# Loads 3 to 4 items ahead, shared score buffers and identity products at the start of an attention and mixture kernel

## The chip, the cores and the metric

One core of one Trainium2 chip. The metric is the device time of one execution in microseconds (us), the median of three runs. Smaller is better.

## The reference

Three layers run one after the other, in float32:

1. Attention for 4 batches of 8 heads, 576 tokens, 64 values for each head. The score of query i and key j is q.k/8 plus a bias, the negative of the decay accumulated from j to i: `bias = -(cum[i] - cum[j])` with `cum = cumsum(max(s, 0))`, capped at 0. Keys after the query are masked, then softmax and the product with v.
2. A gated layer on the 2304 tokens of width 512: `h = (x @ w1) * (x @ w2) @ w3`, then `h @ w_out`, with 1024 inner columns.
3. A soft mixture of 8 experts with 4 slots each: logits against `phi`, a softmax over tokens that forms the slots, a two-layer expert for each slot, a softmax over slots that spreads the results back over the tokens.

## The kernel before

The attention is cut into 32 "items". Items 0 to 7 are the 8 heads of the first batch with query tiles 0 to 2 (64, 128 and 128 queries), items 8 to 15 the same heads with tiles 3 and 4, and items 16 to 31 one head each of the other batches with all five tiles.

The way of an item n: `att_fetch` (line 267) loads q and k, already transposed, into a tile "raw" of two buffers (`NRW`), by the DMAs of lines 278, 279 or 281. `att_prep` (line 284) loads the values v of a pair of heads (line 291, tag "v", two buffers) when the head's number is odd, and four rows that carry the decay into partitions 64 to 67 of the same tile, so that one product yields score and bias. Items 0 and 1 (`NDIR`) get these rows from SBUF (line 300), later ones from a DRAM copy (line 302) that `decay_store` (line 164) has written. Items 0 to 15 (`NF32`) multiply the raw tile in float32; items from 16 on split it into two parts first, in tiles "qa" and "qb" of two buffers each, the same size as "raw". `att_scores` (line 318) makes the product of a query tile (line 334) in a PSUM tile of tag "sg" (four buffers), lets VectorE add the mask and take the row minimum of the scaled negative (line 337) and ScalarE take the exponential (line 342) into the score tile "sc" (three buffers, 1600 columns; tile i begins at column 64 i i, so that tiles 0 to 2 end at column 576). `att_norm` divides by the row sum (VectorE lines 351 and 352, GpSimd line 355). `att_transpose` turns the result on TensorE (lines 370 and 384) and ScalarE copies it out (lines 372 and 386). `att_pv` multiplies a pair of heads with v (through the helper at line 110), and the result is split into two parts of x (lines 419 and 420).

`glu_half` (line 426) multiplies x with w1 and w2 of one block of inner columns (products "gl", line 432). These weights arrive as 64-bit floats, "words": `fetch_words` (line 175, DMA at line 178, three buffers) loads 512 columns, `convert` turns them into 32-bit ones on ScalarE (line 186) and VectorE (lines 189, 190 and 193; another form uses 197, 198 and 201), and `load_words` splits them (ScalarE line 217, GpSimd line 218).

The order: `att_steps` (line 631) lists, for each step n, the scores of item n, the norm and transposes of n-1, the output product of the pair before when n is even, `att_prep` of n+1 and `att_fetch` of n+2. `weave` mixes these lists with the conversion steps and the gated layer's. The sync engine (SP), which issues nearly all loads, works strictly in this program order: a load that waits for its buffer holds back all that follows it. The other engines' instructions are put in order beforehand by a planner, and each engine then runs its own list in that order. Ahead of the steps, the loads of items 0 and 1 and of the first words, the decay rows, `att_prep(0)`, one more word load and the decay store are issued.

Of the kernel before, what the change touches and what calls it, by code (L numbers as in the profile page):

```python
# [10 lines left out]
F32 = mybir.dt.float32  # L11
# [10 lines left out]
P = 128  # L22
B, H, S, D = 4, 8, 576, 64
# [24 lines left out]
def attn_glu_softmoe_kernel(  # L48
# [14 lines left out]
    nc = tc.nc  # L63
# [16 lines left out]
    def psum(tag, name):  # L80
        return ps.tile([P, 512], F32, tag=tag, name=name, bufs=PB[tag])
# [37 lines left out]
    ident = cp.tile([P, P], F32, name="ident")  # L119
# [144 lines left out]
    hd = {}  # L264
    ITEMS = [(h, t) for t in ((0, 1, 2), (3, 4)) for h in range(H)] + [(h, (0, 1, 2, 3, 4)) for h in range(H, NH)]

    def att_fetch(n, ap):
        h, tiles = ITEMS[n]
        if h % 2 == 0:
            b, c = divmod(h // 2, H // 2)  # L270
            for blk, (_, nt, own) in enumerate(BLK):
                if own[0] in tiles:
                    x_t[b, blk, c] = xpl.tile([P, 2, nt], F32R, tag=f"x{blk}", name=f"x_{b}_{blk}_{c}", bufs=NX)
        q0, q1 = QT[tiles[0]][0], sum(QT[tiles[-1]])
        raw = ap.tile([P, 2, S], F32, tag="raw", name=f"raw_{n}", bufs=NRW)
        m = 64 if n < NF32 else P
        if q0:
            nc.sync.dma_start(raw[:m, 0, q0:q1], qk[h, 0, :m, q0:q1])
            nc.sync.dma_start(raw[:m, 1, :q1], qk[h, 1, :m, :q1])
        else:  # L280
            nc.sync.dma_start(raw[:m, :, :q1], qk[h, :, :m, :q1].rearrange("n p t -> p n t"))
        hd[n] = dict(raw=raw, q0=q0, q1=q1)

    def att_prep(n, ap):
        h, tiles = ITEMS[n]
        t = hd[n]
        raw, q0, q1 = t["raw"], t["q0"], t["q1"]
        if h % 2:
            vt = ap.tile([P, 9, 2, D], F32, tag="v", name=f"v_{n}", bufs=VB)
            nv = 2 * tiles[-1] + 1  # L290
            nc.sync.dma_start(vt[:, :nv], v[h // 2, :, :nv])
            t["v"] = hd[n - 1]["v"] = vt
        if n < NF32:
            rows = raw
        else:
            rows = ap.tile([P, 2, S], F32R, tag="qb", name=f"qb_{n}", bufs=QAB)
            qa = ap.tile([P, 2, S], F32R, tag="qa", name=f"qa_{n}", bufs=QAB)
        if n < NDIR:
            for a in range(2):
                nc.sync.dma_start(rows[64 + 2 * a : 66 + 2 * a, :, :q1].bitcast(F32), dec[a][h : h + 1, :, :, :q1])  # L300
        else:
            nc.sync.dma_start(rows[64:68, :, :q1].bitcast(F32), rows_d[h].rearrange("a b n t -> (a b) n t")[:, :, :q1])
        if n < NF32:
            t["mul"] = [rows[:68]]
            return
        rq, rk, qb = raw[:, 0], raw[:, 1], rows
        nc.vector.tensor_copy(qa[:, 0, q0:q1], rq[:, q0:q1])  # L307
        nc.scalar.dma_start(qb[0:64, 0, q0:q1].bitcast(F32), qa[0:64, 0, q0:q1].bitcast(F32))
        nc.vector.tensor_copy(qa[:, 1, :q1], rk[:, :q1])
        nc.gpsimd.tensor_tensor(  # L310
            out=qb[0:64, 1, :q1], in0=rk[0:64, :q1], in1=qa[0:64, 1, :q1].bitcast(F32), op=ALU.subtract
        )
        nc.gpsimd.tensor_tensor(  # L313
            out=qa[64:, 0, q0:q1], in0=rq[64:, q0:q1], in1=qa[64:, 0, q0:q1].bitcast(F32), op=ALU.subtract
        )
        t["mul"] = [qa, qb[:68]]

    def att_scores(n, i, ap):
        t, tiles = hd[n], ITEMS[n][1]
        if i == tiles[0]:  # L320
            t["nmax"] = sm.tile([P, 6], F32, tag="nmax", name=f"nmax_{n}")
            t["rsum"] = rsum_t[n % 3]
            t["sc"] = ap.tile([P, 1600], F32, tag="sc", name=f"sc_{n}", bufs=SCB)
        nmax, rsum, mul = t["nmax"], t["rsum"], t["mul"]
        q0, r = QT[i]
        W = q0 + r

        r = P
        sc = t["sc"][:, 64 * i * i : 64 * i * i + W]
        cuts = [(0, W)] if W <= 512 else [(0, W // 2), (W // 2, W)]  # L330
        for m, (a, z) in enumerate(cuts):
            pp = psum("sg", f"sc_ps_{n}_{i}_{m}")
            for x in mul:
                nc.tensor.matmul(pp[:r, : z - a], x[:, 0, q0 : q0 + r], x[:, 1, a:z], start=x is mul[0], stop=x is mul[-1])  # L334
            m0 = S - P if i == 0 else S - W + a
            last = m == len(cuts) - 1
            nc.vector.tensor_tensor_reduce(  # L337
                out=sc[:r, a:z], in0=pp[:r, : z - a], in1=hd["mask"][:r, m0 : m0 + z - a], scale=-0.125,
                scalar=3.0e38 if m == 0 else nmax[:r, 5:6], op0=ALU.add, op1=ALU.min,
                accum_out=nmax[:r, i : i + 1] if last else nmax[:r, 5:6],  # L340
            )
# [289 lines left out]
    def att_steps(ap):  # L631

        groups = [[] for _ in range(B + 1)]
        N = len(ITEMS)
        for n in range(N + 1):
            tiles = ITEMS[n][1] if n < N else ()
            old = [i for i in ITEMS[n - 1][1] if i] if 0 < n <= N else []
            sc = [(0.2 + 0.3 * i, lambda i=i, n=n: att_scores(n, i, ap)) for i in tiles]
            tr = [(0.2 + 0.3 * i, lambda i=i, n=n: att_transpose(n - 1, i, ap)) for i in old]
            norm = [(0, lambda n=n: att_norm(n - 1))] if 0 < n <= N else []  # L640
            prep = [(0, lambda n=n: att_prep(n + 1, ap))] if n + 1 < N else []
            if n + 2 < N:
                prep += [(0, lambda n=n: att_fetch(n + 2, ap))]
            blks = [k for k in range(2) if BLK[k][2][0] in ITEMS[n - 1][1]]
            pv = [(1.4, lambda n=n, k=k: att_pv(n - 2, k)) for k in blks] if n > 0 and n % 2 == 0 else []
            groups[min(B, max(0, (n - 1) // H))] += [
                *sc[:1], *norm, *sc[1:2], *prep, *sc[2:3], *tr[:1], *sc[3:4], *tr[1:2], *sc[4:], *tr[2:], *pv
            ]
        return groups
# [78 lines left out]
    with tc.tile_pool(name="att", bufs=1) as ap:  # L728
# [49 lines left out]
        prep = [(1, lambda k=k: load(k)) for k in range(2 * N0 + 2)]  # L778
# [323 lines left out]
```

## Time and profile before

| | |
|---|---|
| time, median of 3 runs | 574.28 us (573.58 to 574.37) |
| span of the profiled execution | 569.3 us |
| time outside the span, by the median | 5.0 us |
| TensorE (PE) busy | 519.9 us, 91% |
| VectorE (DVE) busy | 316.7 us, 56% |
| ScalarE (ACT) busy | 311.6 us, 55% |
| GpSimd (POOL) busy | 194.7 us, 34% |
| DMA | 118.04 MB, mean 207 GB/s |

The profile is one execution; its span runs from the first to the last instruction. The profile records no other time for that execution, so the 5.0 us are the difference to the median of the runs. Busy time counts instructions on each engine; PE's weight loads run beside its products. A busy share over the whole span mixes stages with different limits, so the rows further below are taken by stretch.

### The profile page before, as it was taken

The page shows a single profiled execution, that of the slowest core. Times are in us where ns is not written, and L with a number is a line of the kernel's source. Part 1 is how long each engine was busy: PE and PEld are TensorE (multiplying, and loading weights), DVE is VectorE, ACT ScalarE, POOL GpSimd, SP SyncE. Part 2 cuts the span into 40 slices and gives each one's busy share as a digit, 9 for nine tenths or more (in the row PEclk, how much of TensorE's full clock was granted, in tenths as well). Part 3 has the DMA queues.
Part 4 walks back from the last instruction along what each step waited for, and adds up shares of the span by engine and source line. Part 5 has one row for each costly group of instructions (what it writes and reads, how often), then busy time and mean ns, then how long its engine had stood idle before and what let it go on. Part 6 is the DMA issues. An engine that isn't in the chain of part 4 may idle for free.

```text
span 569.3 us, 11835 instructions
## 1 busy us (share of the span) xinstructions
PE 519.9 (91%) x4288; PEld 434.2 (76%) x4288; DVE 316.7 (56%) x966; ACT 311.6 (55%) x845; POOL 194.7 (34%) x247
## 2 busy tenths in 40 slices
PE   1886999788899999999899999999999999999993
PEld 1664788666788897989899879898888999853452
DVE  6558676769987376656565757456640311243333
ACT  4577667666876665845576667456833321321222
POOL 5447531526678456252255444333210000000000
PEclk9998999979999999999999999999999999999997
DMA  6557557657763353536556554465351996689976
GB/s 197 188 164 229 183 180 252 238 170 237 224 218 116 119 165 108 169 95 205 176 155 189 170 185 139 156 200 163 123 212 48 368 411 233 238 295 423 421 296 235
DMA packets 38810, 118.04 MB, mean 207 GB/s; under 512 B 4224, under 2 KB 10560, under 8 KB 35296
## 3 DMA queue, kind: packets, MB, share of 16 engines
q1 hardware_dynamic: 36832, 113.74, 57.9%
q10 hardware_dynamic: 1920, 3.54, 2.5%
q8 instruction: 34, 0.56, 0.4%
q14 instruction: 24, 0.20, 0.1%
HBM read 102.11 MB, written 11.60 MB: 200 GB/s over the span
## 4 chain that ended last, share of the span: by engine, by line
PE 38%; DMA 5%; DVE 4%; ACT 2%; issue 1%; POOL 0%; SPq 0%; DVEq 0%; POOLq 0%; ACTq 0%
PE gl L432 17%; DMA raw_w<-in_w 4%; PE x_ps L110 3%; PE o_ps L1003 3%; PE h_ps L965 3%; PE gn_ps L602 2%; PE sc_ps L334 2%; PE pt_ps L370 2%; PE z_ps L110 1%; DVE w_w L198 1%; PE ptd_ps L384 1%; PE y_ps L889 1%; PE lg L110 1%; DVE sc L337 1%; DVE w_w L201 1%
## 5 line engine op out<-in xcount | busy, mean ns | idle before, releaser
L432 PE MATMUL gl<-x,w12t 128*128 128x320 f32 (+1 forms) x1536 | 241.0, 307 | 4.2 <-DVE nmax L337 2.4
L432 PEld LDWEIGHTS gl<-x,w12t 128*128 128x128 f32 x1536 | 215.4, 194 | 12.8 <-DVE nmax L337 4.3
L342 ACT ACTIVATE sc<-sc,nmax 128x64 f32<-128x64 f32 (+4 forms) x160 | 89.8, 563 | 40.4 <-DVE nmax L337 38.7
L355 POOL TENSOR_SCALAR sc<-sc,rinv 128x64 f32<-128x64 f32 (+4 forms) x160 | 91.0, 585 | 56.7 <-DVE rinv L352 45.8
L313 POOL TENSOR_TENSOR qa<-raw,qa 64x576 fp32r<-64x576 f32 x24 | 36.9, 1536 | 145.5 <-DVE qa L307 134.0
L337 DVE CUSTOM_DVE_ANT_0 sc<-sc_ps,mask 128x64 f32<-128x64 f32 (+4 forms) x160 | 65.3, 424 | 35.6 <-PE sc_ps L334 32.8
L372 ACT COPY pt<-pt_ps 128x128 f32<-128x128 f32 (+3 forms) x128 | 52.4, 422 | 27.8 <-PE pt_ps L370 18.1
L370 PE MATMUL pt_ps<-ident,sc 128*128 128x128 f32 x320 | 56.6, 288 | 5.4 <-POOL sc L355 4.3
L370 PEld LDWEIGHTS pt_ps<-ident,sc 128*128 128x128 f32 x320 | 39.5, 146 | 16.7 <-POOL sc L355 7.7
L334 PE MATMUL sc_ps<-qa 128*128 128x64 f32 (+1 forms) x144 | 46.2, 334 | 5.3 <-DVE nmax L337 2.3
L334 PE MATMUL sc_ps<-raw 68*128 68x288 f32 (+4 forms) x96 | 33.8, 495 | 17.8 <-DMA raw<-rows 13.3
L438 ACT COPY a<-gl 128x256 f32<-128x256 f32 (+1 forms) x64 | 25.4, 397 | 38.4 <-PE gl L432 34.8
L110 PE MATMUL x_ps<-pt,v 128*64 128x256 f32 (+1 forms) x384 | 45.8, 352 | 0.0
L334 PE MATMUL sc_ps<-qb 68*128 68x64 f32 (+1 forms) x144 | 43.7, 307 | 0.7 <-issue 0.7
L310 POOL TENSOR_TENSOR qb<-raw,qa 64x576 fp32r<-64x576 f32 x24 | 38.0, 1582 | 2.2 <-issue 0.5
L974 POOL MEMSET ht<- 128x1024 f32 x2 | 1.9, 954 | 107.3 <-DVE ew L878 98.4
L334 PEld LDWEIGHTS sc_ps<-raw 68*128 68x128 f32 x96 | 19.5, 241 | 23.4 <-issue 12.4
L110 PEld LDWEIGHTS x_ps<-pt,v 128*64 128x64 f32 x384 | 31.1, 139 | 6.9 <-issue 0.9
L186 ACT ACTIVATE w_w<-raw_w 128x512 f32<-128x512 f32 x32 | 21.6, 674 | 23.5 <-DMA raw_w<-in_w 22.4
L420 DVE TENSOR_TENSOR x<-x_ps,x 128x320 fp32r<-128x320 f32 (+1 forms) x32 | 14.0, 453 | 36.5 <-ACT x L419 36.5
L334 PEld LDWEIGHTS sc_ps<-qa 128*128 128x128 f32 x144 | 27.5, 191 | 8.7 <-DVE nmax L337 4.1
L605 ACT COPY gn<-gn_ps 128x512 f32<-128x512 f32 x40 | 22.7, 582 | 15.2 <-PE gn_ps L602 14.8
(180 smaller groups left out, 786.5 us busy)
## 6 DMA issues: line engine op xcount, KB each, us to landing
ew<-in_ew SPq DMA_DIRECT2D x27, 1024.0 KB
raw_w<-in_w SPq DMA_DIRECT2D x32, 512.0 KB
raw<-in_qk SPq DMA_DIRECT2D x24, 576.0 KB
v<-in_v SPq DMA_DIRECT2D x16, 576.0 KB
raw_w3t<-in_w3t SPq DMA_DIRECT2D x16, 512.0 KB
raw_wot<-in_wot SPq DMA_DIRECT2D x8, 512.0 KB
raw_wo<-in_wo SPq DMA_DIRECT2D x8, 512.0 KB
w_d<-w_w SPq DMA_DIRECT2D x8, 512.0 KB
```

The source lines that it names most:

```text
L110: mm = nc.tensor.matmul(out_, lhs, rhs, start=start, stop=stop)
L310: nc.gpsimd.tensor_tensor(out=qb[0:64, 1, :q1], in0=rk[0:64, :q1], in1=qa[0:64, 1, :q1].bitcast(F32), op=ALU.subtract)
L313: nc.gpsimd.tensor_tensor(out=qa[64:, 0, q0:q1], in0=rq[64:, q0:q1], in1=qa[64:, 0, q0:q1].bitcast(F32), op=ALU.subtract)
L334: nc.tensor.matmul(pp[:r, : z - a], x[:, 0, q0 : q0 + r], x[:, 1, a:z], start=x is mul[0], stop=x is mul[-1])
L337: nc.vector.tensor_tensor_reduce(out=sc[:r, a:z], in0=pp[:r, : z - a], in1=hd["mask"][:r, m0 : m0 + z - a], scale=-0.125, scalar=3.0e38 if ...
L342: nc.scalar.activation(out=sc[:r, :W], in_=sc[:r, :W], func=AF.Exp, bias=nmax[:r, i : i + 1], scale=-1.0, accum_out=rsum[:r, i, 0:1],)
L355: nc.gpsimd.tensor_scalar(out=sc, in0=sc, scalar1=rinv[:, i : i + 1], scalar2=1.0, op0=ALU.mult, op1=ALU.mult)
L370: nc.tensor.transpose(tp[:, j * P : (j + 1) * P], sc[:, j * P : (j + 1) * P], ident)
L372: t["turned", i] = nc.scalar.copy(out=pt[:, p0 : p0 + step * (i - 1) + 1 : step], in_=tp[:, : i * P].rearrange("p (j q) -> p j q", q=P))
L432: nc.tensor.matmul(acc[:, :nt], w12_t[fc][:, wi, n, kc], x_t[b, blk, kc][:, xi], start=k == 0, stop=k == 3 * KC - 1)
L438: nc.scalar.copy(out=a_sb[:, :nt], in_=acc[:, :nt])
L605: st["turned", blk, k, h] = nc.scalar.copy(out=gn[:r, 4 * h : 4 * h + 4].rearrange("p c f -> p (c f)"), in_=tp[:r])
```

## The change

Items below 16 keep their raw tile in one of six buffers: those of "raw", "qa" and "qb" in turn. From the start, decay rows are loaded for items 0 to 2 and q and k for items 0 to 3 before the first step; step n then loads the rows of item n+3 and q and k of item n+4 (`FAR` = 3). From item 16 on the old distances hold. The load of the values becomes a function of its own and keeps its place. Among the first eight items, an even and an odd one share a score buffer, the odd one from column 800 on. Ahead of the scores of the first query tile of items 0 to 7, 20 and then 3 each products of the identity with itself are written into the first 128 columns of the PSUM tile that the scores then overwrite.

```
--- before.py
+++ after.py
@@ -83,7 +83,7 @@
 
     NW, NRAW, NG4, NX, NE_ = 8, 3, 4, 6, 11
     NRW, SCB, PTB, QAB, VB = 2, 3, 2, 2, 2
-    NF32, NDIR, ND = 16, 2, 1
+    NF32, NDIR, ND, FAR = 16, 2, 1, 3
 
     A1, CA, CB1, CB, GB1, GB, GC = 0.6, 8, 16, 26, 8, 16, 24
 
@@ -98,6 +98,8 @@
     ]
 
     GROUP = 1000
+
+    IDLE = (20, 3, 3, 3, 3, 3, 3, 3)
 
     CH, OT = ((3, 3, 1, 2), (1, 2, 3, 3)), "wwwweeee"
 
@@ -272,7 +274,8 @@
                 if own[0] in tiles:
                     x_t[b, blk, c] = xpl.tile([P, 2, nt], F32R, tag=f"x{blk}", name=f"x_{b}_{blk}_{c}", bufs=NX)
         q0, q1 = QT[tiles[0]][0], sum(QT[tiles[-1]])
-        raw = ap.tile([P, 2, S], F32, tag="raw", name=f"raw_{n}", bufs=NRW)
+        tag = ("raw", "qa", "qb")[n % 3] if n < NF32 else "raw"
+        raw = ap.tile([P, 2, S], F32, tag=tag, name=f"raw_{n}", bufs=NRW)
         m = 64 if n < NF32 else P
         if q0:
             nc.sync.dma_start(raw[:m, 0, q0:q1], qk[h, 0, :m, q0:q1])
@@ -281,15 +284,18 @@
             nc.sync.dma_start(raw[:m, :, :q1], qk[h, :, :m, :q1].rearrange("n p t -> p n t"))
         hd[n] = dict(raw=raw, q0=q0, q1=q1)
 
+    def att_values(n, ap):
+        h, tiles = ITEMS[n]
+        if h % 2:
+            vt = ap.tile([P, 9, 2, D], F32, tag="v", name=f"v_{n}", bufs=VB)
+            nv = 2 * tiles[-1] + 1
+            nc.sync.dma_start(vt[:, :nv], v[h // 2, :, :nv])
+            hd[n]["v"] = hd[n - 1]["v"] = vt
+
     def att_prep(n, ap):
         h, tiles = ITEMS[n]
         t = hd[n]
         raw, q0, q1 = t["raw"], t["q0"], t["q1"]
-        if h % 2:
-            vt = ap.tile([P, 9, 2, D], F32, tag="v", name=f"v_{n}", bufs=VB)
-            nv = 2 * tiles[-1] + 1
-            nc.sync.dma_start(vt[:, :nv], v[h // 2, :, :nv])
-            t["v"] = hd[n - 1]["v"] = vt
         if n < NF32:
             rows = raw
         else:
@@ -320,7 +326,10 @@
         if i == tiles[0]:
             t["nmax"] = sm.tile([P, 6], F32, tag="nmax", name=f"nmax_{n}")
             t["rsum"] = rsum_t[n % 3]
-            t["sc"] = ap.tile([P, 1600], F32, tag="sc", name=f"sc_{n}", bufs=SCB)
+            if n >= H or n % 2 == 0:
+                t["sc"] = ap.tile([P, 1600], F32, tag="sc", name=f"sc_{n}", bufs=SCB)
+            else:
+                t["sc"] = hd[n - 1]["sc"][:, 800:]
         nmax, rsum, mul = t["nmax"], t["rsum"], t["mul"]
         q0, r = QT[i]
         W = q0 + r
@@ -330,6 +339,9 @@
         cuts = [(0, W)] if W <= 512 else [(0, W // 2), (W // 2, W)]
         for m, (a, z) in enumerate(cuts):
             pp = psum("sg", f"sc_ps_{n}_{i}_{m}")
+            if i == 0 and n < len(IDLE):
+                for _ in range(IDLE[n]):
+                    nc.tensor.matmul(pp[:, :P], ident, ident, start=True, stop=True)
             for x in mul:
                 nc.tensor.matmul(pp[:r, : z - a], x[:, 0, q0 : q0 + r], x[:, 1, a:z], start=x is mul[0], stop=x is mul[-1])
             m0 = S - P if i == 0 else S - W + a
@@ -638,9 +650,13 @@
             sc = [(0.2 + 0.3 * i, lambda i=i, n=n: att_scores(n, i, ap)) for i in tiles]
             tr = [(0.2 + 0.3 * i, lambda i=i, n=n: att_transpose(n - 1, i, ap)) for i in old]
             norm = [(0, lambda n=n: att_norm(n - 1))] if 0 < n <= N else []
-            prep = [(0, lambda n=n: att_prep(n + 1, ap))] if n + 1 < N else []
-            if n + 2 < N:
-                prep += [(0, lambda n=n: att_fetch(n + 2, ap))]
+            prep = [(0, lambda n=n: att_values(n + 1, ap))] if n + 1 < N else []
+            d = FAR if n + FAR < NF32 else 1 if NF32 <= n + 1 < N else 0
+            if d:
+                prep += [(0, lambda m=n + d: att_prep(m, ap))]
+            d = FAR + 1 if n + FAR + 1 < NF32 else 2 if NF32 <= n + 2 < N else 0
+            if d:
+                prep += [(0, lambda m=n + d: att_fetch(m, ap))]
             blks = [k for k in range(2) if BLK[k][2][0] in ITEMS[n - 1][1]]
             pv = [(1.4, lambda n=n, k=k: att_pv(n - 2, k)) for k in blks] if n > 0 and n % 2 == 0 else []
             groups[min(B, max(0, (n - 1) // H))] += [
@@ -744,10 +760,15 @@
         hd["ap"] = ap
         att = att_steps(ap)
         decay_rows()
-        att_prep(0, ap)
+        for n in range(NDIR):
+            att_prep(n, ap)
+        att_fetch(2, ap)
         for k in range(2, NRAW):
             fetch_words(k, ap)
         decay_store()
+        for n in range(NDIR, FAR):
+            att_fetch(n + 1, ap)
+            att_prep(n, ap)
 
         def masks():
```

## Rows read from the trace of the kernel before

**Rows 1.** Windows: length; PE, PEld, DVE, ACT, POOL busy us; clock; DMA; GB/s.

```profile
9.00:46.00 37.00, 28.54 (x145) 21.12 (x146) 23.26 (x86) 24.48 (x79) 17.46 (x26) 1.00 0.61 188
...
46.00:68.00 22.00, 17.15 (x93) 12.74 (x91) 17.33 (x42) 14.38 (x34) 14.47 (x16) 0.84 0.65 200
...
100.00:165.00 65.00, 55.02 (x438) 46.17 (x437) 55.15 (x133) 45.92 (x121) 37.16 (x35) 0.92 0.66 209
...
165.00:460.00 295.00, 288.91 (x2484) 261.17 (x2483) 161.00 (x522) 175.99 (x495) 109.17 (x139) 0.99 0.51 170
```

**Rows 2.** PE's waits, 0 to 46 us: us in total, times, longest.

```profile
PE sc_ps L334 <- DMA raw<-rows: 13.3, 2, 9.6
```

**Rows 3.** SP's waits, 9 to 75 us.

```profile
SPq L278 <- PE sc_ps L334: 11.5, 4, 6.0
...
SPq L291 <- PE x_ps L110: 11.5, 3, 6.2
```

**Rows 4.** SP's loads in time: start us, us, line, out<-in, count.

```profile
6.50 1.85 SPq L300 DMA_DIRECT2D raw<-rows  x2
...
9.91 0.76 SPq L167 DMA_DIRECT2D rows_d<-rows  x1
...
12.09 1.32 SPq L300 DMA_DIRECT2D raw<-rows  x2
...
14.93 0.69 SPq L302 DMA_DIRECT2D raw<-rows_d  x1
...
25.68 0.55 SPq L178 DMA_DIRECT2D raw_w<-in_w  x1
...
32.44 0.33 SPq L291 DMA_DIRECT2D v<-in_v  x1
```

**Rows 5.** PE in time: the scores of items 1, 2, 4 and 5.

```profile
15.79 2.47 PE L334 MATMUL sc_ps<-raw 68*128 68x64 f32 x6 [3.71 <-DMA raw<-rows]
...
18.69 2.36 PE L334 MATMUL sc_ps<-raw 68*128 68x64 f32 x6
...
26.07 2.47 PE L334 MATMUL sc_ps<-raw 68*128 68x64 f32 x6 [0.52 <-DMA raw<-rows_d]
...
35.58 1.33 PE L334 MATMUL sc_ps<-raw 68*128 68x64 f32 x6 [0.43 <-issue]
```

**Rows 6.** PE by shape, 9:33 and 33:46: busy us, mean ns.

```profile
L334 PE MATMUL sc_ps<-raw 68*128 68x320 f32 x10 | 6.4, 741 | 0.0
...
L334 PE MATMUL sc_ps<-raw 68*128 68x320 f32 x6 | 2.1, 432 | 0.0
```

**Rows 7.** PE in narrow windows: one and three products of 128 columns.

```profile
28.33 0.42 PE L384 MATMUL ptd_ps<-ident,sc 128*128 128x128 f32 x1
...
28.33 0.85 PE L384 MATMUL ptd_ps<-ident,sc 128*128 128x128 f32 x3
...
34.61 0.32 PE L384 MATMUL ptd_ps<-ident,sc 128*128 128x128 f32 x1
...
34.61 0.53 PE L384 MATMUL ptd_ps<-ident,sc 128*128 128x128 f32 x3
```

**Rows 8.** POOL in time: the identity.

```profile
2.12 0.28 POOL masks.py:199 TENSOR_SCALAR_AFFINE_SELECT ident<-ident 128x128 f32<-128x128 f32 x1
```

**Rows 9.** DVE's conversions by line, 9.6 to 45.6 and 45.6 to 68 us.

```profile
L193 DVE SCALAR_TENSOR_TENSOR w_w<-raw_w,w_w 128x512 uint32<-128x512 uint32 x8 | 6.0, 746 | 0.0
...
L190 DVE SCALAR_TENSOR_TENSOR w_w<-raw_w,w_w 128x512 int32<-128x512 int32 x7 | 4.8, 688 | 0.1
...
L193 DVE SCALAR_TENSOR_TENSOR w_w<-raw_w,w_w 128x512 uint32<-128x512 uint32 x6 | 5.8, 959 | 0.0
...
L190 DVE SCALAR_TENSOR_TENSOR w_w<-raw_w,w_w 128x512 int32<-128x512 int32 x5 | 4.6, 913 | 0.1
```

**Rows 10.** DVE and POOL in time: two that overlap.

```profile
52.20 1.64 DVE L193 SCALAR_TENSOR_TENSOR w_w<-raw_w,w_w 128x512 uint32<-128x512 uint32 x1
...
51.60 1.69 POOL L218 TENSOR_TENSOR w12t<-w_w,w12t 128x512 fp32r<-128x512 f32 x1
```

More of the change, by code (lines that the diff above doesn't have):

```diff
@@ L100, in attn_glu_softmoe_kernel @@
     GROUP = 1000
+    IDLE = (20, 3, 3, 3, 3, 3, 3, 3)
     CH, OT = ((3, 3, 1, 2), (1, 2, 3, 3)), "wwwweeee"
@@ L274, in att_fetch @@
         q0, q1 = QT[tiles[0]][0], sum(QT[tiles[-1]])
-        raw = ap.tile([P, 2, S], F32, tag="raw", name=f"raw_{n}", bufs=NRW)
+        tag = ("raw", "qa", "qb")[n % 3] if n < NF32 else "raw"
+        raw = ap.tile([P, 2, S], F32, tag=tag, name=f"raw_{n}", bufs=NRW)
         m = 64 if n < NF32 else P
@@ L282, in att_fetch, with att_values @@
         hd[n] = dict(raw=raw, q0=q0, q1=q1)
+    def att_values(n, ap):
+        h, tiles = ITEMS[n]
+        if h % 2:
+            vt = ap.tile([P, 9, 2, D], F32, tag="v", name=f"v_{n}", bufs=VB)
+            nv = 2 * tiles[-1] + 1
+            nc.sync.dma_start(vt[:, :nv], v[h // 2, :, :nv])
+            hd[n]["v"] = hd[n - 1]["v"] = vt
     def att_prep(n, ap):
@@ L287, in att_prep @@
         raw, q0, q1 = t["raw"], t["q0"], t["q1"]
[L288 to L292, printed above, removed]
         if n < NF32:
@@ L322, in att_scores @@
             t["rsum"] = rsum_t[n % 3]
-            t["sc"] = ap.tile([P, 1600], F32, tag="sc", name=f"sc_{n}", bufs=SCB)
+            if n >= H or n % 2 == 0:
+                t["sc"] = ap.tile([P, 1600], F32, tag="sc", name=f"sc_{n}", bufs=SCB)
+            else:
+                t["sc"] = hd[n - 1]["sc"][:, 800:]
         nmax, rsum, mul = t["nmax"], t["rsum"], t["mul"]
@@ L332, in att_scores @@
             pp = psum("sg", f"sc_ps_{n}_{i}_{m}")
+            if i == 0 and n < len(IDLE):
+                for _ in range(IDLE[n]):
+                    nc.tensor.matmul(pp[:, :P], ident, ident, start=True, stop=True)
             for x in mul:
@@ L640, in att_steps @@
             norm = [(0, lambda n=n: att_norm(n - 1))] if 0 < n <= N else []
-            prep = [(0, lambda n=n: att_prep(n + 1, ap))] if n + 1 < N else []
-            if n + 2 < N:
-                prep += [(0, lambda n=n: att_fetch(n + 2, ap))]
+            prep = [(0, lambda n=n: att_values(n + 1, ap))] if n + 1 < N else []
+            d = FAR if n + FAR < NF32 else 1 if NF32 <= n + 1 < N else 0
+            if d:
+                prep += [(0, lambda m=n + d: att_prep(m, ap))]
+            d = FAR + 1 if n + FAR + 1 < NF32 else 2 if NF32 <= n + 2 < N else 0
+            if d:
+                prep += [(0, lambda m=n + d: att_fetch(m, ap))]
             blks = [k for k in range(2) if BLK[k][2][0] in ITEMS[n - 1][1]]
@@ L746, in attn_glu_softmoe_kernel @@
         decay_rows()
-        att_prep(0, ap)
+        for n in range(NDIR):
+            att_prep(n, ap)
+        att_fetch(2, ap)
         for k in range(2, NRAW):
@@ L750, in attn_glu_softmoe_kernel @@
         decay_store()
+        for n in range(NDIR, FAR):
+            att_fetch(n + 1, ap)
+            att_prep(n, ap)
         def masks():
```

2 lines of the change are left out of this document (1 added, 1 removed).

## The prediction

> **What bounds the kernel now.** I read the table of windows first, to see which engine is full in which stretch. From 165 us to 460 us TensorE (PE) is busy 288.91 of 295 us, 98%: that part is bound by PE, and whatever comes before it early or late is handed on to the end. Up to 68 us no engine is full. From 9 to 46 us PE is busy 28.54 of 37 us, VectorE (DVE) 23.26, ScalarE (ACT) 24.48; from 46 to 68 us DVE is the fullest, 17.33 of 22 us, or 79%; from 100 to 165 us it is DVE again, 55.15 of 65 us, or 85% [rows 1]. So the first 68 us are a pipeline that waits for its feed, and the change lies in them.
>
> What it waits for is seen next, in the waits of PE and of the SP queue. PE waits 13.3 us for the decay rows of items 0 and 1 [rows 2]. SP, which issues all loads in program order, stands 11.5 us at line 278, an item's q, until PE has finished an older item's scores (two "raw" buffers), and 11.5 us at line 291, the values, until an older pair's output products are done [rows 3]. All that is queued behind stands with it. The worst case is plain in the order of SP: a word load at 25.68, then nothing until the values go out at 32.44; item 5's decay rows stand behind that load in line 302's place [rows 4]. The scores show the same: items 1, 2 and 4 start at 15.79, 18.69 and 26.07, about 3.4 us for each item, but item 5 starts at 35.58, 9.5 us after item 4 [rows 5].
>
> The third thing is PE's clock. Scores of one shape, 68x320, take 741 ns each from 9 to 33 us and 432 ns from 33 to 46 us [rows 6]. The granted clock stands at 1.00 over both, but the durations are those of the lower level (1.2 GHz) first and the upper one (2.4 GHz) later. I go by the durations.
>
> **The change part by part.** The profiled execution has a span of 569.3 us; 574.28, the median, is 5.0 us more. I take that 5.0 as fixed and move the span.
>
> *Fetch 3 to 4 items ahead.* Nothing is added: the same loads go out in another order, and items below 16 use the four buffers of "qa" and "qb" that only items from 16 on need. With six buffers in place of two, the load of item n+4 needs the scores of item n-2, long done when step n is issued: the waits at lines 278 and 281 for scores go. The wait for values stays, with two buffers; behind it on SP stand words, the rows of item n+3 and the fetch of item n+4, but items 5 and 6 have been sent for by then (their rows in steps 2 and 3, the values of item 5 in step 4). So the 6.2 us from 26.23 to 32.44 [rows 4] no longer holds back item 5: its distance of 9.5 us falls towards 3.4, 6.1 us gained. At the start, item 1's rows are issued right behind item 0's. That pair was issued from 12.09 to 13.41 and its scores began at 15.79, 2.4 us later [rows 4, 5]; issued at 8.4 and over at 9.7 it gives 12.1, 3.7 us earlier. Item 2 gains little: its rows are read back from DRAM, and the store that precedes them, issued until 10.67 [rows 4], now comes behind item 1's two loads, a fetch and the word load, so about 2 us later. With 2.4 us for the store to land, 0.65 to issue and 2.4 to arrive it starts at 18.1 instead of 18.69. Feed alone thus gives item 5 between 0.6 + 6.1 = 6.7 us and 3.7 + 6.1 = 9.8 us.
>
> At item 16 the tags "qa" and "qb" pass to their later users; item 16 gets the buffers of items 10 and 11, whose scores are long done. I cost that at nothing; with the cover gone it would be one load's latency, 2.4 us. The shared score buffer (two items in one tile, 800 columns apart) also costs nothing: item 10 still waits for item 7 at the latest, as before, and items up to 9 for older ones than before.
>
> *Identity products.* Each is a float32 product of 128 columns. Float32 scores appear as two matmuls each (ten of 320 columns for the five items 0 to 4 [rows 6]), and 128 columns take (0.85-0.42)/2 = 0.215 us at the lower clock and (0.53-0.32)/2 = 0.105 us at the upper [rows 7]; no row shows such a product itself, so 0.21 us at full clock and 0.43 us at half are its bounds. The 20 ahead of item 0 need only the identity, ready at 2.40 [rows 8], and fill a PE that idles for the first 9.6 us [rows 2]. At half clock throughout they would end at 2.4 + 40 x 0.215 = 11.0, 1.4 us after item 0's scores could begin. In the trace the level had changed between 28.33 and 34.61 of nearly unbroken work [rows 7], 6.3 us; allowing that, 29 of the 40 run slow and 11 fast, ending at 9.9: 0.3 us late, which I take. The other 21 (3 for each of items 1 to 7) cost 4.5 to 9.0 us of PE. At full clock the 28.54 us of PE work from 9 to 46 fall to some 17 (432/741 of it, since nearly all ran slow) plus 4.5, far under 37: covered by waits for DVE and ACT.
>
> *What is late next.* With feed and clock out of the way it is DVE, whose order mixes scores, norms and word conversions. DVE's work from 9 to 68 us is 23.26 + 17.33 = 40.6 us in 59, 69%. Done at the 79% of 46 to 68 us it takes 51.5 us (7.5 gained); at the 85% of 100 to 165, 47.9 us (11.1). But denser work meets more of GpSimd: the same conversions of line 193 take 746 ns on average until 45.6 us and 959 after, line 190 688 and 913 [rows 9]. Over the 8 and 7 early ones the later means add 1.7 + 1.6 = 3.3 us. I take half of it, 1.65: 42.2 us of work is 53.6 us at 79% (5.4 gained) and 49.8 at 85% (9.2). The middle is 7.3; less the 0.3 of item 0, 7.
>
> One conversion shows what stretches them: the one at 52.20 lasts 1.64 us while a GpSimd subtraction runs from 51.60 to 53.29 [rows 10], so 0.55 us after that ends. The Trainium skill, SBUF — State Buffer, section on engine and AXI ports, says that DVE with two SBUF inputs and a reading GpSimd instruction exclude each other on a shared port pair, the later one blocking fully. The trace agrees in that row. By this rule compressing the stage costs DVE time, which speaks against the change, and by it the first rival below is what happens in full.
>
> The TensorE: Matmul & The Clock Gate page of the Trainium skill, Part 1, puts the clock's ramp under 1% of a typical span, which gives an estimate of at most 5.7 us for the clock by itself, 568.6 at best. The trace shows slow scores to about 33 us [rows 6], off the path for most of that time, so it does not contradict the page; the sum above does not use it.
>
> **Carry.** A 7 us earlier start at 68 us passes through 68 to 165 us, where order and engines' loads are unchanged, to the PE-bound part. Span 569.3 - 7 = 562.3, time 567.3.
>
> **Rivals.** *DVE takes most of it back* (the port): all 3.3 us added, at 79%: 43.9/0.788 = 55.7 us, 3.3 gained, 571.0. For it: DVE is already 79 to 85% full wherever words and items meet. Against: from 9 to 46 us DVE is only 63% full, so there is room for much of the extra time. Chance 0.15.
>
> *The gain is given back from 100 to 165 us*: if DVE's 55.15 us there, and the words behind them on SP, set the time at 165 whatever came before, only noise is left: 574.3. For it: DVE's 85%; against: nothing in that stretch is tied to a clock time, its loads hang on its own conversions. Chance 0.12.
>
> *PE stays at the low level and becomes the bound: slower.* The place is items 2 to 7. If the gap before item 2 lets the clock fall (from 46 to 68 us PE is short of work and its mean clock is 0.84 [rows 1]), the 21 products cost 9.0 us on top of 28.54, 37.6 us in a stretch of 37. At PE's 98% that takes 38.4 us, 1.4 us slower; were PE on the path at every item, up to 9 us. I take 2: 576.3. It decides once PE's work passes 37 us, that is, above 0.40 us for each product with the scores still at 741 ns. Against: 20 dense products come first. Chance 0.13.
>
> **How the numbers follow.** The forecast has 0.60, with its own range 563 to 570. About 0.2%, 1.15 us, is what can be told from no change here. Faster: 0.60 + 0.15 = 0.75. The give-back splits 0.08 same and 0.04 slower; with 0.13, slower is 0.17. The range goes from 561 (11.1 gained plus 2 us that a lost clock drop of 46 to 68 us may return) to 574.5, leaving out the slower cases and a little below.
>
> **What would show it.** Right: item 1 starts near 12, item 5 near 28; no SP wait at lines 278 or 281 in the first 46 us; 68x320 scores at 430 ns from item 1 on; gl products begin some 7 us sooner and the offset stays through 165 us. Wrong: item 5 early but gl not; scores still at 741 ns after item 2, PE over 95% busy; DVE's line 193 above 950 ns from 10 us on; an offset at 68 us that is gone at 165.

## The result, and the profile after

| kernel | median, us | runs, us |
|---|---|---|
| before | 574.33 | 573.58 to 575.59 (4) |
| after | 567.55 | 567.12 to 567.64 (4) |

The ratio is 0.9872, 95% interval 0.9844 to 0.99: 6.8 us faster, where 567.3 us and 7 us were forecast. The size came out, by luck, as will be seen; the place and the cause did not. Ratios, here and below, leave out executions more than 1.5% above the fastest of their kernel, while the medians in the tables count all.

The profiled execution of the changed kernel took 567.64 us with a span of 565.9, so 1.7 us lie outside the span, and 1.7 to 2.0 us do in every later run. The execution that stands ahead of the prediction was therefore a quick one of some 571.0 us (569.3 + 1.7), not one at the median; the kernel before took 570.39 to 582.32 us over the runs that served for comparison. Between the two traces only 3.4 us of span are to be explained; the other 3.4 us of the medians are that.

The table of windows, columns as in [rows 1]; the second and third row are stretches of their own:

```profile
9.00:46.00 37.00, 29.79 (x167) 25.39 (x166) 21.16 (x84) 23.26 (x76) 20.28 (x30) 0.72 0.61 169
...
14.00:18.00 4.00, 0.18 (x2) 0.00 (x0) 2.14 (x9) 2.30 (x8) 0.62 (x2) 0.62 0.59 195
18.00:29.00 11.00, 10.20 (x37) 9.30 (x38) 4.52 (x25) 6.37 (x22) 5.10 (x10) 0.52 0.93 261
...
46.00:68.00 22.00, 19.19 (x133) 15.09 (x132) 18.15 (x44) 15.96 (x42) 11.42 (x9) 1.00 0.86 249
100.00:165.00 65.00, 58.10 (x514) 48.75 (x512) 55.28 (x143) 50.16 (x135) 33.52 (x35) 0.98 0.74 246
165.00:460.00 295.00, 287.44 (x2430) 259.57 (x2431) 153.56 (x506) 171.17 (x480) 105.76 (x136) 0.99 0.47 158
```

PE does 58.10 us from 100 to 165 us where it did 55.02. From 14 to 18 us it has 0.18 us of work, and from there to 29 us the granted clock is 0.52, the lower level (1.2 GHz).

PE in time (start, duration, line, operation): the products, and the first scores of items 1, 2, 4, 5 and 7, which answer to [rows 5].

```profile
2.46 7.45 PE L344 MATMUL sc_ps<-ident 128*128 128x128 f32 x40 [2.46 <-POOL ident masks.py:199]
...
11.50 0.33 PE L346 MATMUL sc_ps<-raw 68*128 68x64 f32 x2
...
18.80 2.48 PE L346 MATMUL sc_ps<-raw 68*128 68x64 f32 x6 [4.63 <-DMA raw<-rows_d]
...
27.26 1.94 PE L346 MATMUL sc_ps<-raw 68*128 68x64 f32 x6
29.70 0.71 PE L346 MATMUL sc_ps<-raw 68*128 68x64 f32 x4
...
38.89 1.41 PE L346 MATMUL sc_ps<-raw 68*128 68x64 f32 x4 [1.64 <-DMA raw<-rows_d]
```

Scores of 68x320 from 16 to 29 us and from 29 to 38 us (count, busy us, mean ns), answering to [rows 6]:

```profile
L346 PE MATMUL sc_ps<-raw 68*128 68x320 f32 x6 | 3.4, 666 | 0.0
...
L346 PE MATMUL sc_ps<-raw 68*128 68x320 f32 x5 | 1.9, 454 | 0.0
```

SP's waits from 0 to 46 us (total, times, longest), and SP in time around the longest, answering to [rows 3, 4]:

```profile
SPq L292 <- PE x_ps L112: 14.4, 2, 9.8
```

```profile
25.30 0.53 SPq L180 DMA_DIRECT2D raw_w<-in_w  x1
35.67 0.33 SPq L292 DMA_DIRECT2D v<-in_v  x1
36.05 0.64 SPq L308 DMA_DIRECT2D raw<-rows_d  x1
```

The waits of q and k for a raw buffer, which an older item's scores set free, are gone from SP. The wait for the values' buffer has grown, from 6.2 us between two issues [rows 4] to 9.8, and item 7's rows, with the next words, stand behind it.

Where the lead is made is read from VectorE's products of the gate (gC, then gT), which mark the progress of the gated projection. Here are the 1st, 7th, 10th and 12th, with some instructions ahead of the 7th to which the text returns. Kernel before, DVE in time:

```profile
69.22 0.49 DVE L450 TENSOR_TENSOR gC<-gl,a 128x320 f32<-128x320 f32 x1 [0.50 <-ACT a L438]
...
112.41 1.84 DVE L201 SCALAR_TENSOR_TENSOR wot<-raw_wot,wot 128x512 int32<-128x512 int32 x1
...
114.70 1.97 DVE L198 SCALAR_TENSOR_TENSOR w3t<-w3t,raw_w3t 128x512 int32<-128x512 int32 x1
116.70 1.11 DVE L201 SCALAR_TENSOR_TENSOR w3t<-raw_w3t,w3t 128x512 int32<-128x512 int32 x1
...
118.16 0.48 DVE L337 CUSTOM_DVE_ANT_0 sc<-sc_ps,mask 128x320 f32<-128x320 f32 x1
...
121.69 0.49 DVE L450 TENSOR_TENSOR gC<-gl,a 128x320 f32<-128x320 f32 x1 [3.04 <-PE gl L432]
...
151.08 0.41 DVE L450 TENSOR_TENSOR gT<-gl,a 128x256 f32<-128x256 f32 x1
...
176.97 0.41 DVE L450 TENSOR_TENSOR gT<-gl,a 128x256 f32<-128x256 f32 x1
```

The changed kernel:

```profile
69.32 0.48 DVE L462 TENSOR_TENSOR gC<-gl,a 128x320 f32<-128x320 f32 x1
...
104.96 1.84 DVE L203 SCALAR_TENSOR_TENSOR wot<-raw_wot,wot 128x512 int32<-128x512 int32 x1
...
111.59 0.69 DVE L203 SCALAR_TENSOR_TENSOR w3t<-raw_w3t,w3t 128x512 int32<-128x512 int32 x1
...
112.47 0.48 DVE L349 CUSTOM_DVE_ANT_0 sc<-sc_ps,mask 128x320 f32<-128x320 f32 x1
...
114.18 0.49 DVE L462 TENSOR_TENSOR gC<-gl,a 128x320 f32<-128x320 f32 x1 [1.21 <-PE gl L444]
...
141.44 0.42 DVE L462 TENSOR_TENSOR gT<-gl,a 128x256 f32<-128x256 f32 x1
...
172.26 0.42 DVE L462 TENSOR_TENSOR gT<-gl,a 128x256 f32<-128x256 f32 x1
```

At 69 us the changed kernel is 0.1 us behind. At the 7th product it is 7.5 us ahead, at the 10th 9.6, at the 12th 4.7. Nothing was gained in the first 68 us that the gate saw; all of the lead is made between 84 us and the 10th product, and half of that is given back by the 12th.

The largest step, 13.0 us from the 6th (at 108.74) to the 7th product before and 7.4 us after (106.79 to 114.18), shows how. Item 16's scores of 320 columns are on PE at 112.28 before and 109.27 after. Before, VectorE's queue holds three word conversions ahead of the eviction of item 16's scores, 1.84, 1.97 and 1.11 us; the first 64 columns leave PSUM by 118.0 and the 320 by 118.6. PE's gate products, which share the tag "sg" with the scores, wait 1.14 us for the first of these and run at the lower level (granted clock 0.50 from 118 to 122 us), twelve in 3.57 us. After, the same evictions stand between and behind conversions of 0.69 us, are over by 112.95, and the twelve gate products go ahead beside them, in 2.00 us. PE in time, before and then after:

```profile
118.01 3.57 PE L432 MATMUL gl<-x,w12t 128*128 128x320 f32 x12 [1.14 <-DVE nmax L337]
```

```profile
112.07 2.00 PE L444 MATMUL gl<-x,w12t 128*128 128x320 f32 x12
```

The length of the three conversions counts as well as their place. Before, GpSimd works almost without a break beside them, from 112.20 to 117.28 us; after, it stands idle from 109.85 to 119.91, and the three conversions that begin at 109.50, 110.84 and 111.59 take 0.90, 0.69 and 0.69 us. That is 2.3 us in place of 4.9, so up to 2.6 of the step's 5.6 us may come from the length; no run separates the two. GpSimd in time, before:

```profile
112.20 1.50 POOL L313 TENSOR_TENSOR qa<-raw,qa 64x576 fp32r<-64x576 f32 x1 [6.01 <-DVE qa L307]
...
115.50 1.78 POOL L355 TENSOR_SCALAR sc<-sc,rinv 128x448 f32<-128x448 f32 x2
```

So the order of VectorE's queue differs, though no edit names it: the planner orders PE, VectorE, ScalarE and GpSimd by itself, and a change of loads gives it another problem. Of the 3440 PE instructions that both kernels have, 586 stand in another place, all within the first 894. The words also come sooner. From 68 to 122 us, VectorE's wait for a converted word half and ScalarE's for the word itself, before:

```profile
DVE wot L198 <- ACT raw_wot L197: 6.4, 4, 2.1
```

```profile
ACT wot L186 <- DMA raw_wot<-in_wot: 7.7, 5, 2.3
```

and after:

```profile
DVE wot L200 <- ACT raw_wot L199: 2.1, 3, 0.9
```

```profile
ACT wot L188 <- DMA raw_wot<-in_wot: 2.5, 2, 1.5
```

Before, SP also stands for raw buffers, 13.4 us at line 278 from 46 to 122 us, with the words behind it:

```profile
SPq L278 <- PE sc_ps L334: 13.4, 4, 6.0
```

After, no wait for score products is left at the lines of q and k.

### The profile page after: what moved, and what is told of

It reads as the page before. It is cut to its first block, busy times and chain, and to the rows that moved or that the text cites. A ratio compares the mean times of both kernels' runs of the same rounds, so it can differ in the third digit from the quotient of the medians.

```text
span 565.9 us, 12007 instructions
## 1 busy us (share of the span) xinstructions
PE 527.7 (93%) x4370; PEld 444.4 (79%) x4370; DVE 313.6 (55%) x966; ACT 311.3 (55%) x845; POOL 197.5 (35%) x247
## 4 chain that ended last, share of the span: by engine, by line
PE 38%; DMA 6%; ACT 3%; DVE 3%; issue 1%; SPq 0%; ACTq 0%; DVEq 0%
PE gl L444 17%; DMA raw_w<-in_w 5%; PE x_ps L112 3%; PE o_ps L1024 3%; PE h_ps L986 3%; PE gn_ps L614 2%; PE z_ps L112 2%; PE pt_ps L382 2%; PE sc_ps L346 1%; PE y_ps L910 1%; PE ptd_ps L396 1%; ACT raw_w L199 1%; ACT sc L354 1%; PE lg L112 1%; ACT w_w L188 1%
## 5 line engine op out<-in xcount | busy, mean ns | idle before, releaser
L444 PE MATMUL gl<-x,w12t 128*128 128x320 f32 (+1 forms) x1536 | 237.7, 304 | 3.3 <-DVE nmax L349 2.7
L444 PEld LDWEIGHTS gl<-x,w12t 128*128 128x128 f32 x1536 | 211.7, 190 | 12.4 <-DVE nmax L349 4.6
L112 PE MATMUL x_ps<-pt,v 128*64 128x256 f32 (+1 forms) x384 | 47.5, 353 | 0.0
L346 PE MATMUL sc_ps<-raw 68*128 68x288 f32 (+4 forms) x96 | 31.6, 455 | 7.4 <-DMA raw<-rows_d 6.8
L346 PEld LDWEIGHTS sc_ps<-qb 68*128 68x128 f32 x144 | 28.2, 196 | 3.0 <-issue 2.8
```

The lines of the kernel that those rows point to most:

```text
L112: mm = nc.tensor.matmul(out_, lhs, rhs, start=start, stop=stop)
L444: nc.tensor.matmul(acc[:, :nt], w12_t[fc][:, wi, n, kc], x_t[b, blk, kc][:, xi], start=k == 0, stop=k == 3 * KC - 1)
```

## The experiments

Each was timed against the kernel before on the same chip; times are medians.

| | kernel | us | before, us | ratio, 95% interval |
|---|---|---|---|---|
| 1 | the kernel before again | 575.94 | 574.96 | 1.0007 (0.9974 to 1.0039) |
| 2 | changed, no identity products | 567.99 | 574.96 | 0.986 (0.9817 to 0.9904) |
| 3 | before, with identity products | 576.89 | 574.96 | 1.002 (0.9989 to 1.0052) |
| 4 | changed, a score buffer per item | 568.07 | 574.96 | 0.9873 (0.9834 to 0.9912) |
| 5 | before, with six raw buffers | 584.58 | 574.66 | 1.0113 (1.0057 to 1.0168) |
| 6 | changed, far fetch for items 0 to 7 alone | 579.3 | 574.66 | 1.007 (1.0035 to 1.0106) |
| 7 | changed, item 2's rows from SBUF too | 580.19 | 574.66 | 1.0039 (0.9987 to 1.0091) |
| 8 | changed, values one step later | 571.07 | 574.66 | 0.9933 (0.9896 to 0.9971) |
| 9 | before's loads in the changed kernel's order | 586.88 | 574.45 | 1.0192 (1.0154 to 1.023) |
| 10 | changed kernel's loads in before's order | 573.01 | 574.45 | 0.9984 (0.9954 to 1.0013) |
| 11 | 7 in the changed kernel's order | 568.89 | 574.45 | 0.987 (0.9827 to 0.9913) |
| 12 | changed, with before's list of steps | 571.62 | 574.42 | 0.9942 (0.9913 to 0.997) |

**1, the kernel before once more**, only a blank added, for its scatter.

> The kernel before, unchanged, profiled once more: its shown span (569.3 us) stands 5.0 us under its median, the changed kernel's 565.9 only 1.7 us under its own. Theory A, the shown profile of before was an unusually quick execution: the new span is near 572.6, 1.7 us under the time, and the first gl result comes later than the 69.2 us of the shown profile, by up to 3 us. Theory B, 5.0 us outside the span belong to this kernel: the span is again near 569.3. Time 574.3 by both.

571.59 to 579.64 us in 12 runs. The kernel before varies by some 8 us from run to run; even 12 runs leave an interval of 0.3% to either side. The trace taken here, of a run of 579.64 us, has a span of 577.8, so 1.8 us lie outside it. Against the other trace of the kernel before it is 1.4 us late at the gate's first product and 2.6 at the 10th, so a lead of that size between two single traces shows nothing.

**2 and 3, the identity products.**

```
-    IDLE = (20, 3, 3, 3, 3, 3, 3, 3)
+    IDLE = ()
```

> The changed kernel without its 41 identity products, loads and score buffers as changed. Theory feed (the gain is the loads sent for ahead, the products add nothing since the clock fell again at 14 us): 565 to 568. Theory clock (the products bring the gain): 572 to 575, scores at 741 ns to beyond 30 us. If both carry a part: 569 to 571.

Kernel 3 is the kernel before with the same tuple and the three lines that issue the products.

> The kernel before with the 41 identity products alone. Theory feed: 574 to 578, since items 2 to 7 still wait for their loads and PE has 4.5 to 9 us more to do. Theory clock: 568 to 571. If both carry a part: 571 to 573.

Taken out they change nothing (567.99 beside 567.55). From item 8 on kernel 2 has the changed kernel's order on every engine, so this comparison is a clean one. Kernel 3 gains nothing either, but the planner moved 647 of its 3440 PE instructions, so it tests the products together with another order.

**4, the score buffers.**

```
-            if n >= H or n % 2 == 0:
-                t["sc"] = ap.tile([P, 1600], F32, tag="sc", name=f"sc_{n}", bufs=SCB)
-            else:
-                t["sc"] = hd[n - 1]["sc"][:, 800:]
+            t["sc"] = ap.tile([P, 1600], F32, tag="sc", name=f"sc_{n}", bufs=SCB)
```

> The changed kernel with a score buffer of its own for every item, three in turn as before. In the changed trace the scores of items 5 to 7 run before the first output product (32.7 us), so they hold six score areas at once. Theory sharing matters: scores stop at item 3 until item 0 is turned, 570 to 573. Rival, DVE and ACT are the bound there and the head start buys nothing: 567 to 568.

No change in the time. But the planner moved over 750 of the PE instructions against the changed kernel, so the run does not show by itself that the sharing costs and brings nothing.

**5 and 6, the buffers alone, and the far fetch for the first eight items alone.** In the kernel before (5), and in the changed kernel (6):

```
-        raw = ap.tile([P, 2, S], F32, tag="raw", name=f"raw_{n}", bufs=NRW)
+        tag = ("raw", "qa", "qb")[n % 3] if n < NF32 else "raw"
+        raw = ap.tile([P, 2, S], F32, tag=tag, name=f"raw_{n}", bufs=NRW)
```

```
-        tag = ("raw", "qa", "qb")[n % 3] if n < NF32 else "raw"
+        tag = ("raw", "qa", "qb")[n % 3] if n < H else "raw"
...
-            d = FAR if n + FAR < NF32 else 1 if NF32 <= n + 1 < N else 0
+            d = FAR if n + FAR < H else 1 if H <= n + 1 < N else 0
...
-            d = FAR + 1 if n + FAR + 1 < NF32 else 2 if NF32 <= n + 2 < N else 0
+            d = FAR + 1 if n + FAR + 1 < H else 2 if H <= n + 2 < N else 0
```

> The kernel before with one change: items 0 to 15 take their raw tile from six buffers in turn. Loads go out in the old order (rows of n+1, q and k of n+2 in step n), no products, own score buffers. Theory W (the waits for a raw buffer held the word loads behind them on SP; free of those, conversions come earlier, and the gain appears from 90 us on): 566 to 570, SP's waits at lines 278 and 281 near 0, the tenth word converted before 55 us. Theory distance (items must be sent for 3 to 4 ahead): 572 to 576.

> The changed kernel with the loads ahead and the six buffers for items 0 to 7 alone; items 8 to 15 go back to two buffers and to the old distances. The prediction's theory (the gain is made by items 0 to 8 before 68 us): 566 to 569. Rival, theory W (it is made by items 8 to 15, whose waits for a buffer hold the words of 50 to 80 us): 572 to 576, with SP waiting 8 us or more at lines 281 and 282 between 45 and 80 us.

Both are slower than the kernel before. Kernel 6 has the whole start of the change, by which the prediction explained the gain, and loses 0.7%. That speaks against the prediction's place, though its order is not that of the changed kernel either. From item 10 on all four engines have the order of kernel 3 in it, which has none of the early loads: 1.007 against 1.002, with intervals that overlap. In that order the early start gains nothing.

**7 and 8, the gap before item 2, and the wait for values.**

```
-    NF32, NDIR, ND, FAR = 16, 2, 1, 3
+    NF32, NDIR, ND, FAR = 16, 3, 1, 3
...
         att_fetch(2, ap)
+        att_prep(2, ap)
...
```

```
-            prep = [(0, lambda n=n: att_values(n + 1, ap))] if n + 1 < N else []
+            prep = [(0, lambda n=n: att_values(n, ap))] if n < N else []
```

> The changed kernel with item 2's decay rows, too, taken from SBUF, ahead of the store. Item 2's scores then start near 13 instead of 18.8 us, and PE's 4.6 us gap in which the clock fell is closed. Theory early start counts: 564 to 566. Rival, the first 60 us are bound by DVE, ACT and the values' two buffers, and a start of items earlier is lost there: 567 to 568.5.

> The changed kernel with the values of a pair asked for one step later in SP's order, so that the wait for one of their two buffers (9.8 us from 25.8 in the changed trace) holds back two rows loads, two fetches and a word less. Theory W extended (words held by the values' wait are the next loss): 564 to 566, the seventh word converted before 40 us instead of 43.3. Rival, the values themselves then come late for the output products: 568 to 571.

Kernel 7 closes the gap: item 2's scores begin at 14.17 us, and the granted clock from 18 to 29 us is 0.85 in place of 0.52. Kernel 8 shortens the wait for the values' buffer, from 14.4 us in two to 8.5 in one up to 46 us. Yet kernel 7 is slower than the changed kernel, and kernel 8 seems so too, by 0.6%, with intervals that overlap a little. The planner again placed the engines' instructions otherwise, which these two can't tell from the loads.

**9 to 11, the order held fixed.** Manual dependencies chain each engine's instructions in a written order. They bind the planner only; no work is added. The numbers in the strings are left out here:

```
+    ORDER = {"PE": "...", "DVE": "...", "Activation": "...", "Pool": "..."}
+    for engine, text in ORDER.items():
+        mine = [x for x in list(nc.cur_bb.bb.instructions) if x.engine == getattr(mybir.EngineType, engine)]
...
+        for a, z in zip(ids, ids[1:]):
+            tc.add_manual_dep(mine[z], mine[a].name, follow, reason="follow")
```

Kernel 9 is bound from item 10's scores on, since its two raw buffers don't allow the changed kernel's order before that; its list of steps has the changed kernel's entries, and items 0 to 7 share score buffers. In 10, which has the list of steps of the kernel before, and in 11 all of the program is bound, 11 to the order of kernel 2, which is the changed kernel's from item 8 on.

> The kernel before (its loads two items ahead, two row buffers, no identity products; items 0 to 7 share score buffers in pairs) with the instructions of PE, VectorE, ScalarE and GpSimd tied from item 10's scores on to the order that they have in the changed kernel. The ties are ordering edges for the planner; no instruction and no wait on the chip is added. Theory 'order' (the gain comes from the order in which the planner places the engines' instructions from about item 10 to item 21, not from loads that arrive sooner): 566 to 570 us, and the lead over the kernel before grows between 84 and 145 us as it does in the changed kernel. Theory 'loads' (the gain needs the rows in the buffers sooner): 573 to 578 us, as before.

> The changed kernel without its identity products, all four engines tied to the order that they have in the kernel before: its loads three to four items ahead, six row buffers and shared score buffers stay. Theory 'order': 573 to 579 us, no lead at 145 us. Theory 'loads': 566 to 569 us, as without the products but with the changed kernel's own order (567.99).

> The changed kernel with item 2's decay rows taken from SBUF too (as in the run with three items, 580.19 us), but the four engines tied to the changed kernel's order. Theory 'order': the 12 us that the run with three items lost were its order, so 565 to 569 us, and item 2's scores near 16 instead of 18.8 us without a gain at the end of more than 1 us. Theory 'loads' (the extra row loads ahead of the first words cost the time): 575 to 582 us again.

| | order of before | order of the changed kernel (upper row: from item 10 on) |
|---|---|---|
| loads of before | 1 | 1.0192 |
| loads of the changed kernel, no products | 0.9984 | 0.986 |

Neither theory holds alone. The new loads in the old order bring 0.2%, within the error; the new order with the old loads costs 1.9%; together they gain 1.4%. Kernel 10 shows the first half of it, DVE and PE in time:

```profile
72.92 0.49 DVE L462 TENSOR_TENSOR gC<-gl,a 128x320 f32<-128x320 f32 x1 [0.50 <-ACT a L450]
...
115.21 1.97 DVE L200 SCALAR_TENSOR_TENSOR w3t<-w3t,raw_w3t 128x512 int32<-128x512 int32 x1
117.21 1.12 DVE L203 SCALAR_TENSOR_TENSOR w3t<-raw_w3t,w3t 128x512 int32<-128x512 int32 x1
...
118.67 0.48 DVE L349 CUSTOM_DVE_ANT_0 sc<-sc_ps,mask 128x320 f32<-128x320 f32 x1
...
122.20 0.49 DVE L462 TENSOR_TENSOR gC<-gl,a 128x320 f32<-128x320 f32 x1 [3.04 <-PE gl L444]
```

```profile
118.52 3.57 PE L444 MATMUL gl<-x,w12t 128*128 128x320 f32 x12 [1.29 <-DVE nmax L349]
```

ScalarE waits 2.9 us for words there, where before it was 7.7:

```profile
ACT wot L188 <- DMA raw_wot<-in_wot: 2.9, 3, 2.3
```

The words are early, and it does not help: the conversions still stand ahead of item 16's eviction, the last two of 1.97 and 1.12 us, and the 7th product comes at 122.20, as before. Kernel 9 shows the other half, DVE's and SP's waits from 46 to 122 us, and DVE in time:

```profile
DVE wot L198 <- ACT raw_wot L197: 10.1, 4, 4.7
DVE sc L343 <- PE ptd_ps L390: 8.0, 1, 8.0
```

```profile
SPq L289 <- PE x_ps L110: 24.4, 5, 11.7
```

```profile
75.31 0.48 DVE L456 TENSOR_TENSOR gC<-gl,a 128x320 f32<-128x320 f32 x1
...
129.23 0.49 DVE L456 TENSOR_TENSOR gC<-gl,a 128x320 f32<-128x320 f32 x1 [0.90 <-PE gl L438]
```

An order that asks for words and scores early makes VectorE stand still where they come late, 10.1 and 8.0 us. Where the binding begins, at item 10's first scores, kernel 9 is 0.9 us behind the kernel before (60.08 against 59.19); at the first product of the gate it is 6.1.

With the early loads the traces repeat by order. The 10th product of the gate comes at 140.78 in kernel 2 and 142.12 in kernel 11, as at 141.44 in the changed kernel; in the order of before it comes at 151.88 in kernel 10, as late as with the old loads, 151.08 and, in kernel 1, 153.64. The giving back repeats too: from the 10th to the 12th product the new order takes 30.8, 31.2, 29.0 and, with the old loads, 30.6 us (changed, 2, 11, 9), the old one 25.9, 25.8 and 25.7 (before, 1, 10).

And kernel 11 is faster than kernel 7 by nothing but the order, 0.987 against 1.0039, some 10 us: kernel 7's loads were not at fault. What item 2's gap costs is not shown by it. The order that it is bound to puts item 0's transposes ahead of item 2's scores, so these begin only at 18.95 us, behind the transposes of the line below, and not near 16 as expected, though their rows come from SBUF. PE in time, kernel 11:

```profile
18.51 0.64 PE L396 MATMUL ptd_ps<-ident,sc 128*128 128x128 f32 x3 [2.93 <-ACT pt L384]
```

**12, where the order came from.** The values are an entry of their own in the list of steps, and some of the last steps have no load left, so the part of the list for items 8 to 15 has 67 entries where it had 63. It is cut at 60% of its number of entries: behind the 40th instead of the 37th, one score step of item 14 later. That moves 128 of PE's instructions in the order as written, which the planner starts from.

```
-            prep = [(0, lambda n=n: att_values(n + 1, ap))] if n + 1 < N else []
+            jobs = [[], []]
+            if n + 1 < N:
+                jobs[0].append(lambda n=n: att_values(n + 1, ap))
...
+            prep = [(0, lambda fs=fs: [f() for f in fs]) for fs, on in zip(jobs, (n + 1 < N, n + 2 < N)) if on]
```

> The changed kernel with the load of the values and the fetch of the decay rows in one entry of the list of steps, as before. In the changed kernel the values are an entry of their own, so the list of items 8 to 15 is longer, the cut at 60% of it and the interleaving with the gate's and the word steps fall elsewhere, and 128 of PE's 3440 instructions are written down in another order (the same 128 between the kernel before and the changed one); here they stand as in the kernel before, and the planner is free. Loads, buffers and identity products stay. Theory 'entry' (the side effect of the longer list gave the planner its better order): 572 to 578 us, as with the order of the kernel before (573.01). Theory 'loads and their own plan' (a plan made for early loads is good whatever the list): 565 to 570 us.

Between both theories: 0.9942, apart from the changed kernel's 0.9872 and from 1. So about half of the gain, 0.7%, hangs on the list of steps, whose cut moved as a side effect; the other half comes with the early loads and the plan that the planner makes for them.

## Why the size was right and the place was not

*What bounds the kernel.* Right that PE is nearly full from 165 us on (287.44 of 295 us). Wrong that the first 68 us are where it is decided; DVE's 85% from 100 to 165 us [rows 1] stood in the prediction and was read as a share, not as an order that could be better.

*Feed.* Item 1 at 11.50 (12.1 said), item 2 at 18.80 (18.1), item 5 at 29.70 (near 28): 5.9 us sooner than [rows 5], a little under the 6.7 to 9.8 that the feed was to give. The waits for raw buffers at the lines of q and k went. But the next item that the values' wait holds back was not looked for. It is item 7, at 38.89, with the words behind. The first output of the attention (x, at line 431) is 3.2 us later than before, because the planner put it behind items 5 and 6: ScalarE copies it at 32.95 us before and at 36.11 after.

*Identity products.* The 20 end at 9.91, as said (9.9), and the first scores then run at 432 ns. The step failed after that: the prediction named the gap before item 2 only in a rival. PE idles 4.63 us there, the clock falls to the lower level, and 68x320 scores take 666 ns until 29 us. The price that this rival gave, 2 us slower, did not come either: PE is busy only 29.79 of 37 us and not on the path. Kernel 2 puts the products at nothing.

*What is late next.* This is the step that failed. It gained 7.3 us by letting VectorE do the same work at 79 to 85%; at 69 us nothing was gained. VectorE's work from 9 to 68 us is 21.16 + 18.15 = 39.3 us in the changed kernel, not denser than before, since its order had been planned anew. In place of "denser" the runs show "otherwise ordered": a lead of 9.6 us at the 10th product that comes with the new order and stays away without it (kernels 1 and 10 against 2 and 11). Its largest step, 5.6 us, is made where conversions no longer stand ahead of item 16's evictions; that this one move makes the gain is argued from the traces, and no run moved it by itself.

From 46 to 100 us the conversions do get longer. Lines 195 and 192, which answer to lines 193 and 190 in [rows 9], before and after:

```profile
L193 DVE SCALAR_TENSOR_TENSOR w_w<-raw_w,w_w 128x512 uint32<-128x512 uint32 x9 | 7.8, 867 | 0.0
L190 DVE SCALAR_TENSOR_TENSOR w_w<-raw_w,w_w 128x512 int32<-128x512 int32 x8 | 7.5, 933 | 0.1
```

```profile
L195 DVE SCALAR_TENSOR_TENSOR w_w<-raw_w,w_w 128x512 uint32<-128x512 uint32 x10 | 12.6, 1261 | 0.2
L192 DVE SCALAR_TENSOR_TENSOR w_w<-raw_w,w_w 128x512 int32<-128x512 int32 x9 | 6.9, 763 | 0.1
```

Line 195 takes 1261 ns instead of 867, line 192 in turn 763 instead of 933. Together 17 conversions in 15.3 us became 19 in 19.5, 0.13 us more for each, or 2.4 us: of the sort that the first rival feared, under its 3.3 us, and paid without losing the gain. The conversion at 104.96 lasts 1.84 us. A GpSimd subtraction runs beside it, from 104.74 to 106.25, and it ends 0.55 us after that, the remainder that [rows 10] showed:

```profile
104.74 1.51 POOL L319 TENSOR_TENSOR qa<-raw,qa 64x576 fp32r<-64x576 f32 x1 [4.40 <-DVE qa L313]
```

The Trainium skill, SBUF — State Buffer, section "SBUF: two separate sides", has a VectorE instruction with two SBUF inputs and a GpSimd one that reads SBUF exclude each other on a shared port pair. The trace agrees in this row too, and by item 16's eviction the new order has VectorE convert mostly while GpSimd stands idle.

*The rivals.* None came as written: the longer conversions (above) did not take the gain, the lead was made mostly from 100 us to the 10th product and half given back only after that, and the low clock came without the bound. The prediction's own sign that it would be wrong did come: item 5 early but the gate's products not.

*Carry.* "Order and engines' loads are unchanged" from 68 to 165 us was the wrong assumption. Most of the PE instructions that moved lie there. Of the 9.6 us at the 10th product 4.7 are left at the 12th. That loss belongs to the new order (it repeats in kernels 2, 9 and 11); which move in it costs the time was not tried.

*Outside the span.* The 5.0 us were the second wrong term: 1.7 is what a run has. By the traces the change gives 3.4 us, and 7 off 569.3 is too much by 3.6; the 3.3 us too many outside it make up for that. Between medians this error drops out, and there 7 stands beside 6.8. That is luck as well: the 7 was worked out from a denser VectorE up to 68 us, which did not come, and the 6.8 is what is left at the end of a lead of 9.6 that came from the order.

*Score buffers and item 16's buffers* at nothing: kernel 4 has the same time without the sharing, but in another order; the second shows no wait in the trace.

Open: why the planner's plans for kernels 5, 6 and 8 do worse was not tried with the order held fixed, nor what each single move within the new order is worth, nor what closing item 2's gap is worth in a good order.

## What to carry to other kernels

Where a planner orders the engines, an edit of loads, buffers or even the number of list entries makes a new plan, and the plan can be worth more than the edit: here 586 PE instructions moved, and two orders for the same loads lay some 10 us apart (kernels 7 and 11). Compare the instruction order of each engine before explaining a difference by waits, and repeat the experiment with the order held fixed; loads and order are judged together, since here either alone gained nothing. And put a profiled execution beside its own time: without it the trace may be that of a run some microseconds off the median.

## What was not expected of the hardware

PE worked almost without a break from 2.46 to 14.18 us, 7.45 us of that on dense products, then had a gap of 4.63 us. The granted clock was 1.00 from 9 to 14 us, 0.75 from 14 to 16 and 0.50 from 16 to 18, and it stayed at 0.52 from 18 to 29 us, though PE was busy all the time from 20 us on. The kernel before spread over 570.39 to 582.32 us in all its runs; the four of the changed one, 567.12 to 567.64, are few, and kernel 2, the same from item 8 on, spread over 564.90 to 569.54 in six.
